# The last products of the feed-forward groups read 128 rows instead of 64, in an mLSTM and channel-mix kernel

## The chip, the core and the metric

The kernel runs on one core of a Trainium2 chip. The core has a matrix engine (TensorE, in the profile PE, with its weight loads as PEld), a vector engine (VectorE, DVE), a scalar engine (ScalarE, ACT), a general engine (GpSimd, POOL), and SyncE (SP), which here only issues DMA transfers. Each engine takes its instructions in the order of the program and waits on semaphores for the others. On-chip data lies in 128 partitions; TensorE multiplies a stationary operand, loaded first, by a moving one, sums over the partitions (the rows of the product), and writes to banks of PSUM. The metric is the device time of one execution in microseconds (us), and less is better.

## What is computed

The first half is a gated linear recurrence with a matrix state for each of 4 x 8 batches and heads, 768 steps, 40 channels a head. The second half is a feed-forward part over the 320 channels of all heads, with a shift by one token:

```python
C = f_stab[:, :, None, None] * C + i_stab[:, :, None, None] * np.einsum('bhd,bhe->bhde', vt, kt)
n = f_stab[:, :, None] * n + i_stab[:, :, None] * kt
h_tilde = np.einsum('bhde,bhe->bhd', C, qt)
denom = np.maximum(np.abs(np.einsum('bhd,bhd->bh', n, qt)[:, :, None]), 1.0)
y[:, :, t] = o * h_tilde / denom
...
xk = mu_k * x + (1.0 - mu_k) * x_prev
xr = mu_r * x + (1.0 - mu_r) * x_prev
k = np.maximum(xk @ w_k, 0.0)
v = k * k @ w_v
r = 1.0 / (1.0 + np.exp(-(xr @ w_r)))
return (r * v).astype(np.float32)
```

Here x is y with the heads side by side, 320 channels wide; w_k is 320 x 1024, w_v 1024 x 320, w_r 320 x 320.

## The kernel before

**Tiling.** The recurrence is cut into chunks of 128 tokens. Two chunks of one batch make a unit of 256 tokens, the step of the feed-forward part; there are 12 units, three per batch. Within a chunk the scores of all heads are products of q and k (`scores`, line 242), weighed by exponentials (`weigh`, 249); `inter` (263) takes what the state brings in, `intra` (283) what the chunk itself gives, `carry` (364) makes the state of the next chunk. `total`, `norm`, `gate`, `outcome` and `twin` finish the chunk's x on VectorE and GpSimd, and `turn` (394) transposes it, so that channels lie on the partitions.

**Two parts of each operand.** TensorE multiplies in a rounded float32 format (float32r), so each operand of the feed-forward part is kept as a high part, rounded to that format, and a low part, the rest. A product is then the sum of three: high by high, low x by high weights, high x by low weights. 320 channels are two tiles of 128 and one of 64. The tile of 64 is stored twice (`twin` for x, the host's `twice` for the weights), and `mix_l` (line 443) makes its third tile in one instruction with `nsel`, a column of 0 for the first 64 partitions and -1 for the others: rows 0 to 63 of `xl[:, 2]` hold the high part of x, rows 64 to 127 the low part. One product of `xl[:, 2]` and `wh[:, 2]` over 128 rows thus holds two of the three terms. The third, high x by low weights, is a product over 64 rows.

`terms` (line 491) lists these products: three for each of the first two tiles, two for the third, eight in all. `ffn_k` (498) makes two such groups for a pair of feature tiles, 16 products of 128x128 by 128x256, into one PSUM bank; there are four pairs a unit. `ffn_r` (534) makes one group of eight, 128 tokens by 320 channels, and runs twice a unit. `ffn_v` (552) has 24 products for each half unit, all over 128 rows. The weights come in as float64 bits and are taken apart on the chip by `size`, `guard`, `bits`, `parts` and `parts_l` in the first third of the program.

**What sets the order.** The order is written out by hand: the calls from line 576 on, each engine taking its part in that order. Units 0 and 1 are interleaved with the preparation of the weights. The loop from line 1062 on handles, for u from 2 to 11, the feed-forward part of unit u, the attention of unit n = u + 1, and the loads and the first scores of unit m = u + 2. On TensorE one pass is: `inter(n, 0)`, `ffn_k(u, 0)`, `intra(n, 0)`, `carry(n, 0)`, `ffn_k(u, 1)`, `scores(n, 1, ...)` twice, `turn(n, 0)`, `ffn_k(u, 2)`, `inter(n, 1)`, `intra(n, 1)`, `carry(n, 1)`, `ffn_r(u, 0)`, `ffn_k(u, 3)`, `ffn_r(u, 1)`, `turn(n, 1)`, `ffn_v(u)` twice, `scores(m, 0, ...)` twice. The first chunk of a batch has no `inter`, the last no `carry`.

**The scores' operands.** From unit 2 on they too are float32r: `split_h` (line 184, ScalarE) and `split_l` (191) take k and q apart, and `restack` (201) puts the parts above each other in tiles `k3` and `q3` of 120 rows by 18 transfers on SyncE's queue, nine for k and nine for q. There is one `k3` and one `q3`, so the transfers for unit m wait until `scores(n, 1, ...)` have read those of unit n. On SyncE a pass is: the output of unit u - 1, the loads of the output gate, q and k of unit m (lines 172, 160, 145), the 18 transfers, and one load of `e` (216).

Of the kernel before, what the change touches and what calls it, by code (L numbers as in the profile page):

```python
# [16 lines left out]
DM, DFF = H * D, 1024  # L17
P = 128
L = 128                # chunk of the recurrence
CPB = S // L           # chunks of a sequence  # L20
U = 256                # tokens of a unit of the feed-forward part
CPU = U // L
UPB = S // U
NU = B * UPB
UF = 2                 # units whose scores come from float32 products
E1 = D + 1             # a head's values with the column of ones
NF = DFF // P
BH = B * H
NEG = -1e30
# a float64 of 2**-127 has these upper 32 bits; read as a float32, such words keep their order  # L30
SMALL = struct.unpack("<f", struct.pack("<I", (1023 - 127) << 20))[0]
# [3 lines left out]
def mlstm_cmix_kernel(ctx: ExitStack, tc, qf, kf, qT, kT, kn, va, og, gi, gf, wk, wr, wv, mu, cmask, out):  # L35
# [8 lines left out]

# [1 line left out]
    gf_sb = p2.tile([BH, S], F32, bufs=1, name="gf_sb")  # L46
# [12 lines left out]

# [1 line left out]
    # M_t, less the sum of f up to t, is what every weight of the chunk is measured  # L61
    # from; R is the running maximum where the chunk starts.
    nm_dram = [dp.tile([BH, L], F32, name=f"nm_{c}") for c in range(CPB)]
# [49 lines left out]
    def columns(c):  # L113
        """the same with the chunk's tokens on the partitions"""
        ar, dg = rows[c]["ar"], rows[c].get("d")
        pt = ps.tile([P, 512], F32, tag="T", bufs=1, name="pt_g")
        for i in range(3):
            T.transpose(pt[:, i * BH:(i + 1) * BH], ar[:, i, :], ident[:BH, :BH])
        if dg is not None:
            T.matmul(pt[:3 * D, 3 * BH:4 * BH], ones[:, :3 * D], dg, start=True, stop=True)  # L120
        A.activation(acol[:, c, :], pt[:, 0:BH], AF.Copy)
        if c == 0:
            # nothing flows in from before the sequence: only the keys' scales
            A.activation(gk[:, c, 1, :], pt[:, 2 * BH:3 * BH], AF.Exp)
        else:
            A.activation(gk[:, c].rearrange("p i x -> p (i x)"), pt[:, BH:3 * BH], AF.Exp)
        if dg is not None:
            A.activation(dec[:, c, :], pt[:3 * D, 3 * BH:4 * BH], AF.Exp)

# [1 line left out]
    units = [{} for _ in range(NU)]  # L131

    def load_s(u, eng):
        if u >= NU:
            return
        t = units[u]
        if u < UF:
            # the first units' scores come from float32 products: nothing to wait for
            t["k3"] = p2.tile([D, H, U], F32, tag="k3", name="k0_sb", bufs=1)
            t["q3"] = p2.tile([D, H, U], F32, tag="q3", name="q0_sb", bufs=1)  # L140
            eng.dma_start(t["k3"], kf[u])
            eng.dma_start(t["q3"], qf[u])
        else:
            t["k"] = p2.tile([3 * D, 3, U], F32, name="k_sb", bufs=1)
            eng.dma_start(t["k"], kT[u])
# [16 lines left out]
    def load_o(u, eng):  # L162
        """the tile of the results of unit u - 2 and of unit u's output gate"""
        if u < 2:
            sg = p2.tile([P, 2 * CPU, DM], F32, name="sg")
            og_sb = units[u]["o"] = sg[:, :CPU, :]
            eng.dma_start(og_sb, og[u])
            return
        units[u - 2]["sg"] = p2.tile([P, 2 * CPU, DM], F32, name="sg")
        if u < NU:  # L170
            units[u]["o"] = units[u - 2]["sg"][:, CPU:, :]
            eng.dma_start(units[u]["o"], og[u])
# [3 lines left out]

    # float32r parts of q and k, stacked so that one product over 120 rows
    # holds kh*qh + kl*qh + kh*ql of a head
    def split_h(u, nm):
# [23 lines left out]

# [1 line left out]
    state = {}  # L205
# [20 lines left out]
    def exps(u, c, h0, h1):  # L226
        """exp(a_s - M_t) for s <= t, with s on the partitions"""
        if u >= NU:
            return
        t, b, cc, _, _ = where(u, c)  # L230
        e = t["e", c]
        for h in range(h0, h1):
            A.activation(e[:, h, :], e[:, h, :], AF.Exp, bias=acol[:, cc, b * H + h:b * H + h + 1])  # L233
# [17 lines left out]
    def inter(u, c):  # L251
        """from the earlier chunks"""
        if u >= NU:
            return
        t, _, cc, cs, _ = where(u, c)
        if cc == 0:
            return
        Cst = state["C"].rearrange("p h x -> p (h x)")
        pX = t["X", c] = ps.tile([P, 512], F32, tag="A", name="pX")
        for g in range(3):  # L260
            w = 3 if g < 2 else 2
            at = slice(g * 3 * E1, (g * 3 + w) * E1)
            T.matmul(pX[:, at], t["q"][:w * D, g, cs], Cst[:w * D, at], start=True, stop=True)  # L263
# [11 lines left out]
    def intra(u, c, h0=0, h1=H):  # L275
        """from this chunk"""
        if u >= NU:
# [19 lines left out]
    def norm(u, c, step):  # L297
        """1 / max(|n.q|, 1)"""
        if u >= NU:
# [33 lines left out]

    # the state of the next chunk
    def carry_in(u, c, eng):
# [51 lines left out]
    def turn(u, c):  # L387
        """to channels on the partitions; the last 64 channels twice"""
        if u >= NU:
            return  # L390
        t = units[u]
        pT = t["T", c] = ps.tile([P, 512], F32, tag="T", bufs=1, name="pT")
        for i in range(3):
            T.transpose(pT[:, i * P:(i + 1) * P], t["x", c][:, i * P:(i + 1) * P], ident)  # L394
# [13 lines left out]

# [1 line left out]
    def change(u, c, eng):  # L410
# [25 lines left out]
    def mix_l(u, nm, eng):  # L436
# [4 lines left out]
        xl = t["xl" + nm] = p2.tile([P, 3, U], F32R, tag="xl" + nm, name="xl" + nm, bufs=1)  # L441
        # rows 0..63: the high part, rows 64..127: the low part
        V.scalar_tensor_tensor(xl[:, 2, :], xh[:, 2, :].bitcast(F32), nsel, xm[:, 2, :], op0=ALU.mult, op1=ALU.add)  # L443
# [8 lines left out]
    def load_w(nm, i, slot, eng):  # L452
        """a piece of float64 weights: their bits, as pairs of words"""
        cut = slice(i * P, (i + 1) * P)
        wh, wl, src = (a[:, :, cut] if nm == "wk" else a[:, i:i + 1, :] for a in W[nm])
        # other spaces than "st" are those that the first unit has no use for yet
        st = p2.tile([*src.shape, 2], I32, tag=slot, name="wst", bufs=2 if slot == "st" else 1)
# [8 lines left out]
    def guard(nm, i, eng):  # L466
        """what is below float32's smallest normal number comes out as zero"""
        wf = pieces[nm, i]["wf"]
        eng.tensor_scalar(wf, wf, SMALL, None, op0=ALU.max)

    def bits(nm, i, step):
        """float32 of a float64: sign and top bit of the exponent stay; 7 bits of it and 23 of the fraction follow"""
        p = pieces[nm, i]
# [8 lines left out]
    def parts(nm, i):  # L482
        """the float32r parts"""
        p = pieces[nm, i]
# [6 lines left out]
    def terms(xh, xl, wh, wl):  # L491
        r = []
        for ct in range(2):
            r += [(xh, wh, ct, P), (xl, wh, ct, P), (xh, wl, ct, P)]
        r += [(xl, wh, 2, P), (xh, wl, 2, 64)]
        return r

    def ffn_k(u, pr):
# [3 lines left out]
        for i in range(2):  # L502
            f = 2 * pr + i
            for n, (xx, ww, ct, rows) in enumerate(tl):
                T.matmul(pk[:, i * U:(i + 1) * U], ww[:rows, ct, f * P:(f + 1) * P], xx[:rows, ct, :],  # L505
                         start=n == 0, stop=n == len(tl) - 1)

    def relu(u, pr):
        t = units[u]
        # the first unit's wait for wv while the second's pass  # L510
        r = t["r", pr] = p2.tile([P, 2, U], F32, tag="r0" if u == 0 else "rl", name="rl", bufs=2 if u else 4)
# [22 lines left out]
    def ffn_r(u, i):  # L534
        t = units[u]
        pr = t["pr", i] = bank(i, "pr")
        tl = terms(t["xhr"], t["xlr"], *W["wr"][:2])
        for m, (xx, ww, ct, rows) in enumerate(tl):
            T.matmul(pr[:, :DM], xx[:rows, ct, i * P:(i + 1) * P], ww[:rows, ct, :],  # L539
                     start=m == 0, stop=m == len(tl) - 1)  # L540
# [5 lines left out]
    def sigmoid(u):  # L546
        """of unit u's r and of unit u + 2's output gate"""
        sg = units[u]["sg"]
# [20 lines left out]

# [1 line left out]
    every = ExitStack()  # L571
    every.enter_context(tc.manual_schedule(engines=None))

    # the first unit's attention, while the weights come in; then its feed-forward part
    # @first
    gate_b(0)
# [483 lines left out]
    scores(3, 0, 0, "S")  # L1060
    # @last
    for u in range(2, NU):
        n, m = u + 1, u + 2
        # @body
        mix(u, "r")
# [94 lines left out]
        exps(m, 0, 6, 8)  # L1160
        # @tail
    result(NU - 1, 1)
# [68 lines left out]
```

## Time and profile before

| what | us |
|---|---|
| median of three runs | 424.5 |
| lowest and highest run | 422.74, 427.61 |
| span of the profiled execution | 427.9 |
| TensorE busy | 397.2 (93%) |
| VectorE busy | 302.4 (71%) |
| ScalarE busy | 235.3 (55%) |
| GpSimd busy | 183.0 (43%) |

Of the profiled execution only the span is given, from the first instruction to the last; it is 3.4 us above the median of the runs. In the rows of the profile, L505 is a line of the kernel and `out<-in` names the tiles; `64*128 64x256` is a stationary operand of 64 rows by 128 columns and a moving one of 64 rows by 256. The timeline gives the start and the duration in us, the engine (PE is TensorE's product, SPq and ACTq are transfers issued by SyncE and ScalarE), the line and the operation; `x16` merges 16 that follow each other; the bracket at the end is the time that the engine was idle before, and who ended it. A product's end is modelled, and consecutive products overlap in the array, so the distance of two starts tells what one costs, not its duration. In the row of the granted clock each digit is a fortieth of the span, 10.7 us, in tenths of full speed.

### The profile page before, as it was taken

The page shows a single profiled execution, that of the slowest core. Times are in us where ns is not written, and L with a number is a line of the kernel's source. Part 1 is how long each engine was busy: PE and PEld are TensorE (multiplying, and loading weights), DVE is VectorE, ACT ScalarE, POOL GpSimd, SP SyncE. Part 2 cuts the span into 40 slices and gives each one's busy share as a digit, 9 for nine tenths or more (in the row PEclk, how much of TensorE's full clock was granted, in tenths as well). Part 3 has the DMA queues.
Part 4 walks back from the last instruction along what each step waited for, and adds up shares of the span by engine and source line. Part 5 has one row for each costly group of instructions (what it writes and reads, how often), then busy time and mean ns, then how long its engine had stood idle before and what let it go on. Part 6 is the DMA issues. An engine that isn't in the chain of part 4 may idle for free.

```text
span 427.9 us, 7136 instructions
## 1 busy us (share of the span) xinstructions
PE 397.2 (93%) x2482; PEld 356.1 (83%) x2482; DVE 302.4 (71%) x589; ACT 235.3 (55%) x472; POOL 183.0 (43%) x204
## 2 busy tenths in 40 slices
PE   1874899878998999999999999999999999999996
PEld 0864788767888989989889889898899898998976
DVE  4366896699868677687677777876776778765611
ACT  3641553257636647638567566485476574763440
POOL 2355773676745361352452532613614426133040
PEclk9999999996589999999999999999999999999999
DMA  6867643547242464733835647448357465400000
GB/s 170 272 181 233 209 130 101 165 153 227 70 139 93 140 206 161 221 131 129 249 128 188 215 128 216 167 142 241 125 170 225 135 197 178 159 33 0 33 1 32
DMA packets 40022, 65.18 MB, mean 152 GB/s; under 512 B 3913, under 2 KB 26497, under 8 KB 39825
## 3 DMA queue, kind: packets, MB, share of 16 engines
q1 hardware_dynamic: 31836, 45.99, 34.5%
q10 hardware_dynamic: 8149, 18.72, 13.4%
q8 instruction: 20, 0.33, 0.3%
q14 instruction: 17, 0.14, 0.1%
HBM read 41.01 MB, written 4.03 MB: 105 GB/s over the span
## 4 chain that ended last, share of the span: by engine, by line
PE 67%; DVE 0%; issue 0%
PE pk L505 24%; PE pv L561 18%; PE pI L283 8%; PE pr L539 7%; PE pS L242 4%; PE pX L263 3%; PE pC L364 2%; PE pT L394 2%; DVE sg L566 0%
## 5 line engine op out<-in xcount | busy, mean ns | idle before, releaser
L505 PE MATMUL pk<-xhk,wkl 128*128 128x256 f32 (+1 forms) x288 | 96.4, 335 | 0.0
L505 PE MATMUL pk<-xlk,wkh 128*128 128x256 f32 x288 | 82.0, 297 | 0.7 <-DVE xlk L443 0.7
L512 ACT ACTIVATE rl<-pk 128x512 f32<-128x512 f32 x48 | 28.6, 597 | 92.3 <-PE pk L505 86.2
L505 PEld LDWEIGHTS pk<-xhk,wkl 128*128 128x128 f32 (+1 forms) x288 | 58.4, 203 | 14.0 <-issue 2.7
L505 PE MATMUL pk<-xhk,wkh 128*128 128x256 f32 x192 | 66.8, 348 | 0.0
L233 ACT ACTIVATE e<-e,acol 128x128 f32<-128x128 f32 x192 | 59.0, 389 | 5.7 <-POOL e L223 5.5
L561 PE MATMUL pv<-wvh,kh 128*128 128x320 f32 x192 | 60.5, 315 | 1.4 <-DVE sg L566 1.4
L223 POOL TENSOR_SCALAR_AFFINE_SELECT e<-e 128x1024 f32<-128x1024 f32 x24 | 27.0, 1128 | 77.9 <-DMA e<-nm 54.1
L505 PEld LDWEIGHTS pk<-xlk,wkh 128*128 128x128 f32 x288 | 59.4, 206 | 0.9 <-DVE xlk L443 0.9
L561 PE MATMUL pv<-wvl,kh 128*128 128x320 f32 x192 | 59.3, 309 | 0.0
L561 PE MATMUL pv<-wvh,kl 128*128 128x320 f32 x192 | 59.3, 309 | 0.0
L283 PE MATMUL pI<-va_sb,e 128*128 128x41 f32 x384 | 55.1, 309 | 1.8 <-DVE e L249 1.1
L283 PEld LDWEIGHTS pI<-va_sb,e 128*128 128x128 f32 x384 | 52.8, 219 | 4.2 <-DVE e L249 1.4
L522 POOL TENSOR_TENSOR kk<-rl 128x512 f32<-128x512 f32 x25 | 27.0, 1082 | 53.9 <-ACT rl L512 45.8
L505 PEld LDWEIGHTS pk<-xhk,wkh 128*128 128x128 f32 x192 | 39.2, 204 | 9.0 <-issue 3.0
L527 POOL TENSOR_TENSOR kl<-kk,kh 128x512 fp32r<-128x512 f32 x22 | 31.4, 1426 | 31.1 <-DVE kk L522 21.1
L561 PEld LDWEIGHTS pv<-wvh,kh 128*128 128x128 f32 x192 | 36.1, 188 | 1.9 <-DVE sg L566 1.6
L249 DVE TENSOR_TENSOR e<-pS,e 128x512 f32<-128x512 f32 x48 | 31.9, 679 | 7.9 <-PE pS L242 6.9
L561 PEld LDWEIGHTS pv<-wvl,kh 128*128 128x128 f32 x192 | 36.1, 188 | 0.0
L561 PEld LDWEIGHTS pv<-wvh,kl 128*128 128x128 f32 x192 | 36.0, 188 | 0.0
L426 DVE SCALAR_TENSOR_TENSOR xm<-xd,mu_sb,xT 128x256 f32<-128x256 f32 x72 | 35.5, 548 | 0.7
L522 DVE TENSOR_TENSOR kk<-rl 128x512 f32<-128x512 f32 x23 | 20.4, 886 | 17.4 <-ACT rl L512 17.4
(114 smaller groups left out, 786.4 us busy)
## 6 DMA issues: line engine op xcount, KB each, us to landing
e<-nm SPq DMA_DIRECT2D x13, 512.0 KB
e<-nm ACTq DMA_DIRECT2D x11, 512.0 KB
k<-sp_hk SPq DMA_DIRECT2D x40, 120.0 KB
q<-sp_hq SPq DMA_DIRECT2D x40, 120.0 KB
out<-sg SPq DMA_DIRECT2D x12, 320.0 KB
q_sb<-qT SPq DMA_DIRECT2D x10, 360.0 KB
va_sb<-va ACTq DMA_DIRECT2D x10, 328.0 KB
k_sb<-kT SPq DMA_DIRECT2D x9, 360.0 KB
```

The source lines that it names most:

```text
L223: G.affine_select(e, e, pattern=[[0, H], [1, L]], compare_op=ALU.is_ge, fill=NEG, base=0, channel_multiplier=-1)
L233: A.activation(e[:, h, :], e[:, h, :], AF.Exp, bias=acol[:, cc, b * H + h:b * H + h + 1])
L242: T.matmul(pS[:, hh * L:(hh + 1) * L], t["k3"][:, h, cs], t["q3"][:, h, cs], start=True, stop=True)
L249: V.tensor_tensor(ev, t["S", c, half], ev, op=ALU.mult)
L283: T.matmul(t["I", c][:, h * E1:(h + 1) * E1], t["e", c][:, h, :], t["va"][:, c, h * E1:(h + 1) * E1], start=True, stop=True)
L426: V.scalar_tensor_tensor(xm[:, ct, :], t["xd"][:, ct, :], mu_sb[:, i, ct:ct + 1], t["xT"][:, ct, :U], op0=ALU.mult, op1=ALU.add)
L505: T.matmul(pk[:, i * U:(i + 1) * U], ww[:rows, ct, f * P:(f + 1) * P], xx[:rows, ct, :], start=n == 0, stop=n == len(tl) - 1)
L512: A.activation(r.rearrange("p i t -> p (i t)"), t["pk", pr], AF.Relu)
L522: eng.tensor_tensor(kk, t["r", pr], t["r", pr], op=ALU.mult)
L527: eng.tensor_tensor(kl, t["kk", pr], t["kh", pr].bitcast(F32), op=ALU.subtract)
L539: T.matmul(pr[:, :DM], xx[:rows, ct, i * P:(i + 1) * P], ww[:rows, ct, :], start=m == 0, stop=m == len(tl) - 1)
L561: T.matmul(t["pv", i][:, :DM], xx[:, f % 2, ts], ww[:, f, :], start=f == 0 and n == 0, stop=f == NF - 1 and n == 2)
```

## The change

The last product of each group, until now `xh` by `wl` over rows 0 to 63 of the third tile, becomes `xl` by `wl` over all 128 rows. Rows 0 to 63 of `xl[:, 2]` are the high part of x, so this holds the same term; rows 64 to 127 add a further one, the low part of x by the low part of the weights. Those weight rows are there already, since the last 64 channels of the weights are stored twice and `parts_l` makes the low part of the whole tile. The number of rows goes out of the lists of `terms`, and the slices by it go out of the two loops. The other lines of the diff drop comments.

```diff
     def terms(xh, xl, wh, wl):
         r = []
         for ct in range(2):
-            r += [(xh, wh, ct, P), (xl, wh, ct, P), (xh, wl, ct, P)]
-        r += [(xl, wh, 2, P), (xh, wl, 2, 64)]
+            r += [(xh, wh, ct), (xl, wh, ct), (xh, wl, ct)]
...
+        r += [(xl, wh, 2), (xl, wl, 2)]
         return r
...
-            for n, (xx, ww, ct, rows) in enumerate(tl):
-                T.matmul(pk[:, i * U:(i + 1) * U], ww[:rows, ct, f * P:(f + 1) * P], xx[:rows, ct, :],
+            for n, (xx, ww, ct) in enumerate(tl):
+                T.matmul(pk[:, i * U:(i + 1) * U], ww[:, ct, f * P:(f + 1) * P], xx[:, ct, :],
                          start=n == 0, stop=n == len(tl) - 1)
...
-        for m, (xx, ww, ct, rows) in enumerate(tl):
-            T.matmul(pr[:, :DM], xx[:rows, ct, i * P:(i + 1) * P], ww[:rows, ct, :],
+        for m, (xx, ww, ct) in enumerate(tl):
+            T.matmul(pr[:, :DM], xx[:, ct, i * P:(i + 1) * P], ww[:, ct, :],
                      start=m == 0, stop=m == len(tl) - 1)
```

96 products of `ffn_k` and 24 of `ffn_r` are of that kind, 120 of TensorE's 2482. Each engine has as many instructions as before, in the same order. On TensorE, at the end of the first group of `ffn_k(0, 0)`, there stood (xhk and xlk are the high and low parts of x for the keys, wkh and wkl those of w_k):

```order
28 L505 MATMUL pk<-xlk,wkh 128x256
29 L505 MATMUL pk<-xhk,wkl 128x256
30 L505 MATMUL pk<-xlk,wkh 128x256
31 L505 MATMUL pk<-xhk,wkl 128x256
32 L505 MATMUL pk<-xhk,wkh 128x256
```

and now, two lines further down in the file:

```order
28 L507 MATMUL pk<-xlk,wkh 128x256
29 L507 MATMUL pk<-xhk,wkl 128x256
30 L507 MATMUL pk<-xlk,wkh 128x256
31 L507 MATMUL pk<-xlk,wkl 128x256
32 L507 MATMUL pk<-xhk,wkh 128x256
```

Row 31, the last of the group, reads xlk in place of xhk; nothing else moved.

## The prediction

> **What bounds the kernel now.** I read the page first, then the waits of TensorE, the chain of waits, busy time by stretch, the groups by form, and last the timelines of TensorE, SyncE and ScalarE in single units. The page, cut to three lines:
>
> ```profile
> span 427.9 us, 7136 instructions
> ...
> PEclk9999999996589999999999999999999999999999
> ...
> PE 67%; DVE 0%; issue 0%
> ```
>
> The waits of TensorE from 100 us to the end are one row (who waited for whom, us in total, times, longest). Two rows of busy time by stretch follow it: length, then busy us and instructions of PE, PEld, DVE, ACT, POOL, then the granted clock, the DMA share and GB/s.
>
> ```profile
> PE pv L561 <- DVE sg L566: 1.4, 1, 1.4
> ```
>
> ```profile
> 251.20:280.60 29.40, 29.40 (x208) 26.61 (x207) 22.73 (x45) 18.38 (x36) 11.56 (x13) 1.00 0.55 176
> 90.00:120.00 30.00, 28.84 (x127) 24.87 (x126) 28.08 (x51) 18.84 (x44) 21.91 (x21) 0.67 0.49 152
> ```
>
> After 100 us TensorE waits once, for 1.4 us. In one unit of the loop (251.2 to 280.6) it is busy all 29.40 us at full clock, while VectorE, the next busiest, has 22.73. The chain that ended last runs on TensorE almost alone. So a microsecond taken from TensorE's stream is a microsecond of time, until something else is late. Before the loop it is different: from 90 to 120 VectorE is busy 28.08 of 30 us and TensorE's clock averages 0.67.
>
> **What a product over 64 rows costs.** Busy time hides it, since a waiting array counts as busy. It shows in the starts. Timeline of TensorE in a unit (start, duration, then the operation):
>
> ```profile
> 260.31 0.28 PE L505 MATMUL pk<-xhk,wkl 128*128 128x256 f32 x1
> 260.43 0.28 PE L505 MATMUL pk<-xlk,wkh 128*128 128x256 f32 x1
> 260.64 0.38 PE L505 MATMUL pk<-xhk,wkl 64*128 64x256 f32 x1
> 260.95 0.39 PE L505 MATMUL pk<-xhk,wkh 128*128 128x256 f32 x1
> 261.17 0.28 PE L505 MATMUL pk<-xlk,wkh 128*128 128x256 f32 x1
> 261.29 0.29 PE L505 MATMUL pk<-xhk,wkl 128*128 128x256 f32 x1
> ...
> 261.98 0.38 PE L505 MATMUL pk<-xhk,wkl 64*128 64x256 f32 x1
> 262.29 1.98 PE L283 MATMUL pI<-va_sb,e 128*128 128x41 f32 x16
> ```
>
> Products over 128 rows start 0.12 us apart (260.31 to 260.43, 261.17 to 261.29). Around the 64-row product the three steps are 0.21, 0.31 and 0.22: 0.74 where 0.36 would do, so 0.38 us lost. Where a float32 product follows (262.29) I count only the two steps 0.21 and 0.31 against 0.24: 0.28. The receptance products, 320 wide, show the same:
>
> ```profile
> 275.16 0.31 PE L539 MATMUL pr<-wrl,xhr 128*128 128x320 f32 x1
> 275.31 0.30 PE L539 MATMUL pr<-wrh,xlr 128*128 128x320 f32 x1
> ...
> 276.11 0.28 PE L505 MATMUL pk<-xlk,wkh 128*128 128x256 f32 x1
> ```
>
> The three steps from 275.31 to 276.11 take 0.80 where 0.15 + 0.15 + 0.12 = 0.42 would do: 0.38 again. Is it the row count, or the place at the end of an accumulation group? The value products have group ends too, between 254.48 and 254.63:
>
> ```profile
> 254.34 0.31 PE L561 MATMUL pv<-wvl,kh 128*128 128x320 f32 x1
> 254.48 0.31 PE L561 MATMUL pv<-wvh,kl 128*128 128x320 f32 x1
> 254.63 0.31 PE L561 MATMUL pv<-wvh,kh 128*128 128x320 f32 x1
> 254.78 0.31 PE L561 MATMUL pv<-wvl,kh 128*128 128x320 f32 x1
> ```
>
> There the step is 0.15 as everywhere in that stage, so a group's end costs nothing and the row count is what is left.
>
> [...]
>
> **The change, part by part.** It adds and removes no instruction, and no engine's order changes. The last product of each group reads all 128 rows, and takes x from the tile that the product before it reads, so it waits for nothing new. Its own price: no row has this operand pair; the nearest is any 128-row product of the same width, 0.12 or 0.15 us, and a 64-row price of nothing extra is excluded by the rows above. I take 0.12 and 0.15. That the high part of x is released one product earlier (0.12 us) is worth nothing while ScalarE waits for VectorE there.
>
> A unit has eight 64-row products in its key part and two in its receptance part. Five key products are followed by products of the same kind (0.38 each) and three not (0.28): 2.74 us. The receptance pair adds 0.38 + 0.28. Together 3.4 us per unit, of about 29.
>
> What is late next: the scores of the unit after next. SyncE rebuilds k3 and q3 with 18 transfers per unit, and the loop closes on itself (scores, products, split on ScalarE, transfers, scores). Rows of three units, SyncE, TensorE and ScalarE apart:
>
> ```profile
> 269.51 4.88 SPq L201 DMA_DIRECT2D k<-sp_hk  x6
> 281.93 2.39 SPq L201 DMA_DIRECT2D q<-sp_lq  x3
> 311.67 2.39 SPq L201 DMA_DIRECT2D q<-sp_lq  x3
> 339.38 2.39 SPq L201 DMA_DIRECT2D q<-sp_lq  x3
> ```
>
> ```profile
> 287.53 0.34 PE L242 MATMUL pS<-q,k 120*128 120x128 f32 x2
> 316.28 0.34 PE L242 MATMUL pS<-q,k 120*128 120x128 f32 x2
> 344.97 0.45 PE L242 MATMUL pS<-q,k 120*128 120x128 f32 x3
> ```
>
> ```profile
> 268.65 0.83 ACT L184 ACTIVATE sp_hk<-k_sb 120x768 fp32r<-120x768 f32 x1
> 298.38 0.85 ACT L184 ACTIVATE sp_hk<-k_sb 120x768 fp32r<-120x768 f32 x1 [0.25 <-DMA k_sb<-kT]
> ```
>
> ```profile
> SPq L1225 <- DMA out<-sg: 1.8, 1, 1.8
> ```
>
> The last issue ends at 284.32, 314.06 and 341.77 (start plus 2.39), and the scores start at 287.53, 316.28 and 344.97: 3.21, 2.22 and 3.20 later. Part of that is the landing: above 0, at most 2.22 (the second unit did not wait); the nearest row is the wait for the last output to land, 1.8, which I take. Slack is then 1.41, 0.42 and 1.40 us, less than the 3.4 by which TensorE comes earlier. But the rebuilding starts earlier too: it follows the split (268.65 + 0.83, then 269.51), which follows the second pair of key products, and two pairs come before it in a unit: 2 x (0.38 + 0.28) = 1.3 us. Only if TensorE set the split: in the second unit it waited for the load of k (0.25), and then nothing is gained. So the units save 2.7, 0.4 to 1.7, and 2.7 us: 1.9 to 2.4 on average, of which I take 2.2. The rest, 1.2 us, becomes a wait of TensorE at the scores. Eight units have such a successor: 8 x 2.2 = 17.6. The last two have none: 2 x 3.4 = 6.8.
>
> Before the loop, 12 of the 96 key products run at the low clock:
>
> ```profile
> L505 PE MATMUL pk<-xhk,wkl 64*128 64x256 f32 x96 | 38.9, 405 | 0.0
> ```
>
> ```profile
> 112.68 0.41 PE L505 MATMUL pk<-xlk,wkh 128*128 128x256 f32 x1
> 113.02 0.58 PE L505 MATMUL pk<-xhk,wkl 64*128 64x256 f32 x1
> ...
> 113.91 0.41 PE L505 MATMUL pk<-xlk,wkh 128*128 128x256 f32 x1
> 114.12 0.41 PE L505 MATMUL pk<-xhk,wkl 128*128 128x256 f32 x1
> ```
>
> (12 because the mean 405 ns lies an eighth of the way from 380 to 580.) There the three steps from 112.68 take 1.23 against 3 x 0.21: 0.60 lost, 1.04 in a pair, 6.2 in six pairs; two further pairs and four receptance groups at 0.66 and 0.33 add 2.6. How much of these 8.8 us counts depends on VectorE, which waits for TensorE at two late places:
>
> ```profile
> 83.56 0.50 DVE L374 TENSOR_TENSOR Cn<-pC,cm_sb 120x328 f32<-120x328 f32 x1 [2.38 <-PE pC L364]
> 122.46 0.50 DVE L293 TENSOR_TENSOR t<-pI,t 128x328 f32<-128x328 f32 x1 [2.31 <-PE pI L283]
> ```
>
> Bounds 0 and 8.8; between these waits VectorE is nearly full (28.08 of 30), so I take the two waits: 4.7.
>
> Sum: 17.6 + 6.8 + 4.7 = 29.1 us. The span of the profiled execution, 427.9, becomes 398.8; the runs' median is 424.5, so 395.4, say 395.
>
> **The rivals.**
> - All of it comes through: the landing takes less than 1.8 us and the split always follows TensorE. 8 x 3.4 + 6.8 + 4.7 = 38.7, so 386. Against it: slack of 2.22 us at most in the second unit is below 3.4.
> - The load of k sets every split, as at 298.38; then only the slack is saved, (1.41 + 0.42 + 1.40)/3 = 1.1 per unit: 8.6 + 6.8 + 4.7 = 20.1, so 404. Against it: one row in three shows that wait.
> - The change does nothing: 64 rows cost what 128 cost, and the loss belongs to something else in those places that stays, the group's end for one. Then the sum is 0 and the time 424.5. The rows at 254.48 speak against it.
> - Slower: the new waits at the scores lower TensorE's clock. The rows ahead of the slow stretch:
>
> ```profile
> 97.11 0.38 PE L505 MATMUL pk<-xlk,wkh 128*128 128x256 f32 x1 [0.66 <-DVE xlk L443]
> 99.64 0.28 PE L283 MATMUL pI<-va_sb,e 128*128 128x41 f32 x1 [0.50 <-DVE e L249]
> ```
>
> Two short waits, then 0.67 of the clock over 30 us: some 20 us at half. Steps are 0.21 there against 0.12, so such a stretch costs 20 x (1 - 0.12/0.21) = 8.6 us. One gives 404, and from four on (34.4 against 29.1) the kernel is slower: 430 and more. Against it: the 1.4 us wait after 100 us was followed by full clock. [...]
>
> **How the numbers follow.** The forecast 0.55, all through 0.12, load of k 0.18, no effect 0.05, clock 0.10 (one or two stretches 0.06, three 0.01, four or more 0.03). From 385 to 406 lie the forecast, the second rival, half of the first and one stretch of low clock: about 0.82. About 1% is what a measurement of this kernel can tell from no change. Faster by more: 0.55 + 0.12 + 0.18 + 0.06 = 0.91; within 1%: 0.06; slower: 0.03.
>
> **What would show it.** After: steps of 0.12 and 0.15 us through every key and receptance group; a pair of key products in about 1.9 us; a unit of about 26.7 us; TensorE waiting about 1 us per unit for the rebuilt k or q at its scores, and no longer 29.40 of 29.40 busy. Steps still above 0.2 around the last product would refute the first step; no wait at the scores would give the first rival; a clock below 1 after 135 us the last.

## The result and the profile after

| | median, us | lowest and highest, us |
|---|---|---|
| kernel before, same chip | 426.01 | 422.74, 427.61 |
| changed kernel | 400.97 | 398.64, 403.43 |

The ratio is 0.950, with a 95% interval of 0.938 to 0.962: faster by 25 us, inside the range of the prediction, 6 us above its number. The profiled execution took 403.43 us. Four lines of its page follow: span, busy time, granted clock, and the chain that ended last by engine.

```profile
span 401.6 us, 7136 instructions
...
PE 347.7 (87%) x2482; PEld 336.8 (84%) x2482; DVE 317.4 (79%) x589; ACT 234.4 (58%) x472; POOL 190.2 (47%) x204
...
PEclk9999999958779999999999999999989999999999
...
PE 39%; DMA 8%; DVE 6%; ACT 5%; SPq 4%; issue 3%; POOL 2%; ACTq 0%; POOLq 0%
```

TensorE holds 39% of the chain, where it held 67%. In the row of the clock the low slices before the loop remain, and one 8 stands in the loop, at 291 to 301 us. Busy time by stretch for eight units of the loop, in the kernel before and then in the changed one; the stretch begins with the fifth of a chunk's eight score products and ends with the first of such a chunk, at the same two places of both programs (length, then busy us and instructions of PE, PEld, DVE, ACT and POOL, then the granted clock):

```profile
143.05:374.35 231.30, 231.30 (x1617) 209.02 (x1616) 174.42 (x338) 145.58 (x276) 88.51 (x98) 1.00 0.56 178
```

```profile
135.02:355.08 220.06, 206.96 (x1616) 202.19 (x1615) 186.93 (x338) 144.91 (x276) 92.17 (x98) 0.99 0.57 185
```

TensorE's stream got 231.30 - 206.96 = 24.3 us shorter, and 220.06 - 206.96 = 13.1 us of it came back as waits: 11.2 us are left. The 26.3 us of span (427.9 - 401.6) divide so, by these starts:

| part | predicted, us | measured, us |
|---|---|---|
| up to the scores at 143.05, now 135.02 | 4.7 | 8.0 |
| eight units | 17.6 | 11.2 |
| the rest, from 374.35, now 355.08 | 6.8 | 7.0 |

Timeline of TensorE in a unit of the changed kernel:

```profile
261.15 0.28 PE L507 MATMUL pk<-xlk,wkh 128*128 128x256 f32 x1
261.27 0.28 PE L507 MATMUL pk<-xlk,wkl 128*128 128x256 f32 x1
261.39 0.31 PE L541 MATMUL pr<-wrh,xhr 128*128 128x320 f32 x1
261.53 0.30 PE L541 MATMUL pr<-wrh,xlr 128*128 128x320 f32 x1
...
262.26 0.31 PE L541 MATMUL pr<-wrh,xlr 128*128 128x320 f32 x1
262.40 0.30 PE L541 MATMUL pr<-wrl,xlr 128*128 128x320 f32 x1
263.80 0.44 PE L394 MATMUL pT<-ident,x 128*128 128x128 f32 x2 [1.09 <-POOL x L326]
264.91 0.33 PE L394 MATMUL pT<-ident,x 128*128 128x128 f32 x1 [0.68 <-DVE x L332]
```

The step around the last key product (`xlk,wkl`) is 0.12 us and around the last receptance product 0.15, as the prediction took them. What is new stands in the brackets: the transposes of the unit's second chunk wait 1.09 + 0.68 us. The waits of TensorE from 130 us on (who waited for whom: us in total, times, longest):

```profile
PE pT L394 <- POOL x L326: 6.0, 5, 1.9
PE pT L394 <- DVE x L332: 5.4, 8, 0.7
PE pS L242 <- DMA q<-sp_lq: 0.8, 3, 0.3
PE pC L364 <- ACT xT L406: 0.7, 1, 0.7
```

The scores, where the prediction had put the new wait, wait 0.8 us in all. The transposes, which did not wait in the loop before, wait 11.4. Why they do is in the chain of waits, here from one unit into the next (start, duration, what; "issue" is time for which no releaser shows):

```profile
273.83 0.49 DVE sg L568
...
274.37 0.37 SPq L570
...
275.78 7.60 DMA k_sb<-kT
...
283.49 0.86 ACT sp_hk L184
...
284.36 0.51 DVE sp_lk L191
...
285.73 1.10 DVE kk L524
...
288.54 1.84 POOL sp_lq L191
...
291.25 0.82 POOL x L326
...
292.09 1.09 DVE x L332
...
293.23 0.33 PE pT L394
```

SyncE's queue issues the output of the unit before (L570) only when VectorE has made it (`sg`), and the loads of the next unit stand behind it. The load of k lands 7.6 us later, and ScalarE splits k then. VectorE takes the low part (`sp_lk`, from 284.36 us), and the work of the second chunk, which stands behind it in VectorE's order, starts at 285.24. GpSimd's product `x` follows, behind its split of q (`sp_lq`, 1.84 us), then VectorE's copy (`twin`), then the transpose. ScalarE's wait for this load is one row of its waits in the changed kernel, after 130 us (in the kernel before it was 0.2 us, once):

```profile
ACT sp_hk L184 <- DMA k_sb<-kT: 6.3, 5, 2.4
```

The copy is a second lengthening. The groups by form, of the kernel before and then of the changed one (count, busy us, mean ns):

```profile
L332 DVE COPY x<-x 128x64 f32<-128x64 f32 x11 | 2.1, 194 | 5.9 <-POOL x L326 5.9
```

```profile
L332 DVE COPY x<-x 128x64 f32<-128x64 f32 x11 | 10.8, 979 | 5.9 <-POOL x L326 5.8
```

The same copy went from 0.19 to 0.98 us in the mean, and the transpose behind it waits for it in eight passes, up to 0.7 us each: the 5.4 us above. Timeline of GpSimd and VectorE in the unit shown above:

```profile
263.70 1.04 POOL L524 TENSOR_TENSOR kk<-rl 128x512 f32<-128x512 f32 x1
263.77 1.08 DVE L332 COPY x<-x 128x64 f32<-128x64 f32 x1 [0.51 <-POOL x L326]
```

It starts behind GpSimd's square (`kk`) and ends 0.1 us after it. In the kernel before the square came behind the copy (308.15 and 307.89 us in such a unit), when its input `rl` was ready later. There the copy took 0.20 us; beside the square it takes 1.08. What makes it longer isn't shown by these rows.

### The profile page after: what moved, and what is told of

Read it like the earlier page. It is cut to its first block, busy times and chain, and to the rows that moved or that the text cites. A ratio compares the mean times of both kernels' runs of the same rounds, so it can differ in the third digit from the quotient of the medians.

```text
span 401.6 us, 7136 instructions
## 1 busy us (share of the span) xinstructions
PE 347.7 (87%) x2482; PEld 336.8 (84%) x2482; DVE 317.4 (79%) x589; ACT 234.4 (58%) x472; POOL 190.2 (47%) x204
## 4 chain that ended last, share of the span: by engine, by line
PE 39%; DMA 8%; DVE 6%; ACT 5%; SPq 4%; issue 3%; POOL 2%; ACTq 0%; POOLq 0%
PE pk L507 13%; PE pv L563 13%; DMA k_sb<-kT 5%; PE pI L283 5%; SPq L201 3%; PE pr L541 3%; PE pS L242 3%; PE pC L364 2%; PE pX L263 1%; ACT e L233 1%; DMA q<-sp_lq 1%; POOL x L326 1%; DVE x L332 1%; ACT rl L514 1%; DMA e<-nm 1%
## 5 line engine op out<-in xcount | busy, mean ns | idle before, releaser
L507 PE MATMUL pk<-xlk,wkh 128*128 128x256 f32 x288 | 79.7, 290 | 0.5 <-DVE xlk L443 0.5
L223 POOL TENSOR_SCALAR_AFFINE_SELECT e<-e 128x1024 f32<-128x1024 f32 x24 | 30.5, 1272 | 97.2 <-DMA e<-nm 91.9
L507 PE MATMUL pk<-xhk,wkh 128*128 128x256 f32 x192 | 59.0, 307 | 0.0
L507 PEld LDWEIGHTS pk<-xlk,wkh 128*128 128x128 f32 x288 | 57.2, 199 | 0.7 <-DVE xlk L443 0.7
L507 PE MATMUL pk<-xhk,wkl 128*128 128x256 f32 x192 | 55.9, 291 | 0.0
L283 PE MATMUL pI<-va_sb,e 128*128 128x41 f32 x384 | 52.7, 301 | 3.6 <-DVE e L249 2.3
L283 PEld LDWEIGHTS pI<-va_sb,e 128*128 128x128 f32 x384 | 51.6, 215 | 4.6 <-DVE e L249 1.7
L524 POOL TENSOR_TENSOR kk<-rl 128x512 f32<-128x512 f32 x25 | 27.8, 1113 | 31.2 <-ACT rl L514 24.3
L529 POOL TENSOR_TENSOR kl<-kk,kh 128x512 fp32r<-128x512 f32 x22 | 33.5, 1523 | 14.8 <-DVE kk L524 8.4
L507 PEld LDWEIGHTS pk<-xhk,wkl 128*128 128x128 f32 x192 | 38.1, 199 | 0.0
L394 PE MATMUL pT<-ident,x 128*128 128x128 f32 x72 | 15.8, 307 | 25.8 <-DVE x L326 7.8
```

The lines of the kernel that those rows point to most:

```text
L223: G.affine_select(e, e, pattern=[[0, H], [1, L]], compare_op=ALU.is_ge, fill=NEG, base=0, channel_multiplier=-1)
L283: T.matmul(t["I", c][:, h * E1:(h + 1) * E1], t["e", c][:, h, :], t["va"][:, c, h * E1:(h + 1) * E1], start=True, stop=True)
L507: T.matmul(pk[:, i * U:(i + 1) * U], ww[:, ct, f * P:(f + 1) * P], xx[:, ct, :], start=n == 0, stop=n == len(tl) - 1)
L524: eng.tensor_tensor(kk, t["r", pr], t["r", pr], op=ALU.mult)
L529: eng.tensor_tensor(kl, t["kk", pr], t["kh", pr].bitcast(F32), op=ALU.subtract)
```

## The experiments

**Is it the row count? 96 rows.** The last product reads 96 rows instead of 128. It leaves out low x by low weights for 32 of the last 64 channels.

```diff
-        r += [(xl, wh, 2), (xl, wl, 2)]
+        r += [(xl, wh, 2, P), (xl, wl, 2, 96)]
```

> The changed kernel, but the last product of each group reads 96 rows (of the third tile rows 0 to 95), not 128. Theory 1, the loss belongs to the form of 64 rows: steps around the last product stay 0.12 and 0.15 us, the time is that of the changed kernel, about 401 us (ratio 0.95). Theory 2, any product over fewer rows than the one before it costs the restart: steps of 0.21, 0.31 and 0.22 us come back, the time is that of the kernel before, about 425 us.

Measured: 401.15 us, ratio 0.950 (0.941 to 0.960), the changed kernel's own. Its timeline of TensorE:

```profile
250.51 0.28 PE L507 MATMUL pk<-xlk,wkh 128*128 128x256 f32 x1
250.62 0.28 PE L507 MATMUL pk<-xlk,wkl 96*128 96x256 f32 x1
250.74 0.28 PE L507 MATMUL pk<-xhk,wkh 128*128 128x256 f32 x1
```

Steps of 0.11 and 0.12: reading fewer rows than the neighbours cost nothing by itself here. The first theory holds, and the extra time belongs to the form with 64.

**Two 64-row products side by side.** In the kernel before, the second group of each key pair begins with its 64-row product, so that the two of a pair are neighbours. The result stays the same sum.

```diff
-            for j, (...) in enumerate(tl):
+            for j, (...) in enumerate(tl[-1:] + tl[:-1] if i else tl):
```

> The kernel before, with its 64-row products, but in the second group of each pair of key groups the 64-row product comes first instead of last, so that two of them stand side by side. Theory 1, the cost is in going from 128 rows to 64 and back: a pair has two such passages instead of four, saves about 0.28 us, 4 x 0.28 = 1.1 us a unit, and the time falls by some 8 to 12 us, to about 415. Theory 2, every 64-row product has its own price: nothing falls, 426 us, and the second of two neighbours starts 0.3 us after the first.

Measured: 409.54 us, ratio 0.969 (0.961 to 0.977). Its timeline of TensorE:

```profile
250.53 0.28 PE L505 MATMUL pk<-xlk,wkh 128*128 128x256 f32 x1
250.74 0.50 PE L505 MATMUL pk<-xhk,wkl 64*128 64x256 f32 x2
251.16 0.39 PE L505 MATMUL pk<-xhk,wkh 128*128 128x256 f32 x1
251.39 0.28 PE L505 MATMUL pk<-xlk,wkh 128*128 128x256 f32 x1
```

Four steps take 0.86 us where 4 x 0.12 = 0.48 would do: 0.38 is lost, once for two products. So the price is paid in passing from the form with 128 rows to that with 64 and back, not for each product. Not one 64-row product less runs here, and two thirds of the change's gain are there: 16.6 us against 426.15, the median of the kernel before that was measured with it. That is more than the first theory expected, since the stage before the loop gains in full (the scores that started at 143.05 us start at 134.29).

**One product less.** The changed kernel without the last product of each group. It leaves out high x by low weights for the last 64 channels.

```diff
-        r += [(xl, wh, 2), (xl, wl, 2)]
+        r += [(xl, wh, 2)]
```

> The changed kernel without the last product of each group; left out is the high part of x by the low weights of the last 64 channels. That takes 8 x 0.12 + 2 x 0.15 = 1.3 us of TensorE's work from each of 12 units. Theory 1, in the loop TensorE now waits for the x of the second chunk at the transposes (turn): there nearly nothing is gained, only the stage before the loop and the last unit give 2 to 4 us, about 398 us, and the waits at the transposes grow by about 1 us a unit. Theory 2, TensorE's own work still sets the time: 12 x 1.3 = 15 us less, about 386 us.

Measured: 399.39 us, ratio 0.945 (0.936 to 0.954): 96 products of 0.12 us and 24 of 0.15, 15 us in all, are gone, and the time is within 2 us of the changed kernel's. Its longest row of TensorE's waits from 130 us on:

```profile
PE pT L394 <- POOL x L326: 12.4, 8, 2.2
```

The transposes wait for GpSimd's `x` twice as long (12.4 against 6.0), and the eight units take 351.60 - 132.45 = 219.2 us against 220.1. The loop is no longer set by TensorE; the chain ahead of the transpose sets it, as the first theory had it. A part of the missing gain is the clock's: this profile has three stretches of 3.4 us at half clock in the loop where the changed kernel's has one (mean granted clock 0.951 against 0.966), some 3 us more (3.4 x (1 - 0.15/0.26) = 1.4 us each).

**The copy on GpSimd.** In the changed kernel the second chunk's copy is made by GpSimd, behind the product that it reads.

```diff
-        twin(n, 1, V)
+        twin(n, 1, G)
```

> The changed kernel, but in the loop the copy of the second chunk's last 64 channels (twin) is GpSimd's, right behind the product that makes them, instead of VectorE's. In the changed kernel VectorE's copy takes 1.08 us beside GpSimd's square, and the third transpose waits 0.68 us in each pass. Theory 1, these transposes set the loop: that wait goes, 0.5 to 0.7 us a pass, and the time falls by 3 to 6 us to 395 to 398 us. Theory 2, the rebuilding of k and q for the scores sets it (the forecast's): the wait moves to the scores, which then wait about 0.7 us a pass, and the time stays at 401 us.

Measured: 400.69 us, ratio 0.948 (0.938 to 0.958): no gain where the first theory expected one. The wait for the copy is gone, but the one for `x` stays, and the scores wait 2.1:

```profile
PE pT L394 <- POOL x L326: 7.8, 6, 2.7
```

The copy alone isn't the cause. This profile too has three stretches of 3.4 us at half clock in the loop (mean granted clock 0.947), so a gain of some 3 us may be hidden behind them.

**The load of k early.** In the changed kernel SyncE issues the load of k at the head of the pass, ahead of the output that waits for VectorE.

```diff
         n, m = u + 1, u + 2
 
+        load_s(m, SY)
         mix(u, "r")
...
         gate(n, 0, V)
-        load_s(m, SY)
```

> The changed kernel, but in the loop SyncE issues the load of k for unit m at the head of the pass, ahead of the output of unit u - 1 and the loads of the output gate and q, where it waits for nothing of this pass. In the changed kernel ScalarE waits 6.3 us in all, in 5 passes, for that load before it splits k, and the chain of the longest pass goes through it. Theory 1, the load of k sets the loop: that wait goes to 0, and the time falls by 4 to 8 us to 393 to 397 us. Theory 2, it is only one of several things that are late together: the wait goes, the waits at the transposes stay within 3 us of the 13.7 us of the changed kernel, the time stays at 399 to 402 us.

Measured: 393.51 us, ratio 0.933 (0.930 to 0.937), the time that the first theory gave. ScalarE's row for `k_sb` is gone from its waits after 130 us. Waits of TensorE there:

```profile
PE pT L394 <- DVE x L332: 5.4, 8, 0.7
PE pT L394 <- POOL x L326: 3.1, 5, 1.2
PE pS L242 <- DMA q<-sp_lq: 0.5, 2, 0.4
```

But 8.5 us of waits are left at the transposes, of 11.4; that they would fall by less than 3 us is what the second theory had. The load is one of several links. The eight units take 345.52 - 131.69 = 213.8 us by the starts of the scores, against 220.1 in the changed kernel and 216.6 and 219.0 in two further executions (the repeat below and the one with 96 rows).

**The rebuilding late.** The changed kernel with the copy on GpSimd and, so that GpSimd's `x` comes sooner, the low part of q, all nine transfers of q and the load of `e` behind them moved behind `square(u, 3, G)`.

```diff
-        split_l(m, "q", G)
-        restack(m, "q", SY)
-        fetch_m(m, 1, SY)
...
-        twin(n, 1, V)
+        twin(n, 1, G)
...
         square(u, 3, G)
+        split_l(m, "q", G)
+        restack(m, "q", SY)
+        fetch_m(m, 1, SY)
```

> The changed kernel with the copy twin on GpSimd as in the run before, and in the loop GpSimd's split of q (1.84 us, beside which VectorE's 8-element maximum takes 1.77 us) moved behind the second chunk's x and the last square. Theory 1, the chain from the second chunk's sums through VectorE and GpSimd to the transposes sets the loop: it gets shorter by 1.5 to 2 us a pass, the waits at the transposes nearly vanish, the time falls to 390 to 394 us. Theory 2, the rebuilding of k and q sets it: the transposes stop waiting, but the scores wait 1 us or more a pass, and the time stays above 397 us.

Measured: 411.47 us (403.84 to 414.76), without a ratio, since the runs lie too far apart. The theory that it would gain fell: the lowest run, too, is above the changed kernel's 400.97. The profile is of the highest run, 414.76. Waits of TensorE from 130 us on, and its stretch to 412:

```profile
PE pS L242 <- DMA q<-sp_lq: 7.3, 16, 1.1
PE pC L364 <- ACT xT L406: 3.1, 2, 2.8
PE pT L394 <- POOL x L326: 1.2, 2, 0.6
```

```profile
130.00:412.00 282.00, 265.56 (x1974) 260.26 (x1972) 207.26 (x380) 167.59 (x324) 113.45 (x123) 0.95 0.47 150
```

The wait that the prediction had put at the scores appears here, because the rebuilding was made late; and the clock averages 0.95 over 282 us, some 27 us of them at half (four stretches in the timeline, of 3.4, 6.8, 13.7 and 3.4 us). With steps of 0.21 us for 0.12 there, the clock costs 27 x (1 - 0.12/0.21) = 12 us, about what parts this run from the lowest. That the transposes wait 1.2 us for `x`, against 7.8 with the copy moved alone, speaks for GpSimd's split of q as a further link of their chain; it isn't shown, since TensorE now also comes to them later, by its waits at the scores.

**Load, copy and rebuilding together**, and the same three moves on the kernel before. The edits are those of the last two experiments, the early load and the late rebuilding.

> The changed kernel with all three moves: load of k at the head of the pass, twin on GpSimd, split of q behind the last square. Theory 1, both chains that end at TensorE get shorter, so TensorE sets the loop again: waits after 130 us under 5 us in all, units of about 25.6 us, 382 to 388 us. Theory 2, the rebuilding of k and q (18 issues, 14.8 us) is a floor of its own: the scores wait about 1 us a pass, 392 us or more.

> The kernel before, with its 64-row products, and the same three moves. Theory 1, in the kernel before TensorE hides both chains: the moves gain nothing beyond 1%, 422 to 428 us. Theory 2, the moves are worth something by themselves: as much as between the changed kernel and its version with the three moves.

Measured: 393.89 us on the changed kernel, ratio 0.931 (0.923 to 0.938), no better than the early load alone: the transposes no longer wait, the scores do (6.2 us, 16 times), as the second theory had it. On the kernel before 427.04, ratio 1.014 (1.009 to 1.018): slightly slower. While TensorE's own stream is longer than these chains, moving them gains nothing; what they are worth now was opened by the change.

**The changed kernel again, the load with the copy, and a version to keep.** The last one also splits the high part of k ahead of `relu(u, 1)` on ScalarE, now that the load lands early.

```diff
+        split_h(m, "k")
         relu(u, 1)
...
         inter(n, 1)
-        split_h(m, "k")
```

> The changed kernel once more, as the measure for the two runs beside it: 399 to 403 us by both theories. If short stretches at half clock come with long waits of TensorE, its profile shows them only right behind passes in which the transposes waited 2 us or more.

> The changed kernel with the load of k at the head of the pass and the copy twin on GpSimd, the split of q left in its place. Theory 1, the transposes alone still set the loop: 388 to 391 us, since the 5.4 us that they wait for VectorE's copy in the run with the early load go. Theory 2, the rebuilding of k and q for the scores is as late as they are (its last transfer lands within 0.4 us of the scores in that run): the time stays at 392 to 395 us and the scores wait about 0.5 us a pass.

> The same with one more move: ScalarE splits k ahead of the relu of the second pair of key products, not behind its square, so that the 18 transfers start as soon as the scores have read the old tiles, about 1.2 us earlier. Theory 2, the rebuilding sets the loop: its last transfer lands 1 us earlier, the scores stop waiting, and the time falls to 383 to 388 us. Theory 1, the transposes set it: no more than 2 us against the run beside it.

Measured together: the changed kernel 400.17 us, ratio 0.941 (0.929 to 0.954); load and copy 392.19, ratio 0.926 (0.915 to 0.936); with the split 389.19 (386.62 to 393.0), ratio 0.917 (0.906 to 0.928). The repeat had one short stretch of half clock, behind waits of 1.07 + 0.68 us, less than the 2 us that were expected ahead of one. In the load with the copy the eight units take 342.91 - 132.11 = 210.8 us; the wait for the copy is gone, the transposes still wait 3.4 us for `x`, and the scores now wait 1.4 us (6 times). The last version starts the rebuilding sooner by the early split. Its waits of TensorE after 130 us:

```profile
PE pT L394 <- POOL x L326: 4.4, 4, 1.5
```

It lies just above what the second theory gave it, 3.0 us below load and copy. Its scores never wait, and the eight units take 340.44 - 131.54 = 208.9 us; 8 x 3.4 less than before would be 231.3 - 27.2 = 204.1. This version beats both kernels: 37 us below the kernel before that was measured with it (426.48).

## Why the prediction was right in sign and too large by four microseconds

**The price of a 64-row product** (0.38 us, or 0.28 ahead of a float32 product) was right. The steps became 0.12 and 0.15; 96 rows cost as little as 128; and two 64-row products side by side share one price. In the best version, whose loop has no stretch of low clock, TensorE is busy 203.6 of the 208.9 us of eight units, 27.7 less than 231.3, where 8 x 3.4 = 27.2 was taken. The rival that the change does nothing is refuted. What costs is the change between the two forms (0.38 us, once for a single product and once for two side by side), not the number of rows.

**8 x 2.2 = 17.6 for the loop** measured 11.2, and this is the step that failed, in its last sentence: "The rest, 1.2 us, becomes a wait of TensorE at the scores." I followed one chain, the rebuilding of k and q, took its slack as what limits the gain, and left the others unpriced. The one that was late first ends at the second chunk's transpose: load of k, split on ScalarE, low part on VectorE with the chunk's normalization queued behind it, the product `x` on GpSimd, copy, transpose. The waits there came to 11.4 us over the loop, and 0.8 at the scores. Taking away the load's part gave 7 us by medians (393.51 against 400.97 and 400.17), which were measured beside different medians of the kernel before; by the ratios, 0.933 against 0.950 and 0.941, it is 3 to 7 us. By the traces it is 2.8 to 6.3 us of the eight units, and 219.0 - 213.8 = 5.2 against the run with 96 rows, where neither has a stretch of low clock. The copy on top gave 213.8 - 210.8 = 3.0 there, and nothing that could be seen by itself, with the load still late and more low clock. What makes the transposes wait for `x` with the load early (3.1 us, and 3.4 with the copy moved too) wasn't separated; GpSimd's split of q is the next suspect.

My chain was not wrong, only second: with the transposes' chain shortened the scores wait (1.4 us, and 6.2 with the rebuilding moved back, which makes it later by itself), and with the split early no wait is left at the scores.

**Rivals.** "The load of k sets every split" had the right mechanism and the wrong reach: it gave 404 by way of the rebuilding, in every unit, while the load delayed ScalarE in 5 passes and, in the unit whose chain is shown, did its harm by VectorE's queue. That all comes through is refuted for the change alone; the best version comes within 4.8 us of it in the eight units. The clock did fall behind new waits, in stretches of 3.4 to 13.7 us and not of 20: one of 3.4 in the profiled execution, at about 1.4 us, and 27 us in the kernel with the late rebuilding. In its profile the change alone lost little by it.

**Before the loop** 4.7 was taken and 8.0 measured, inside its bounds of 0 and 8.8. The two pairs of key products between 67 and 82 us went in steps of 0.21 us before, the step at half clock (0.21 at 113.91); now they run between 66 and 73 us in steps of 0.12. The row of the clock doesn't show this (1.00 from 66 to 82 us in the kernel before), and up to 93 us it can't be relied on: in the kernel before the receptance products go in steps of 0.27 up to 93.05 us and of 0.15 from 93.28 on, both under a 9. VectorE, which I had counted as the cover, is busy 39.8 of the 40 us from 60 to 100 us, where it was 33.2. That it got its inputs earlier is what I take from it; no run shows it alone. Every kernel without the lone 64-row key products has the scores that started at 143.05 us at 131.5 to 135.0, and the other one with them at 139.37. What brings the short steps sooner there wasn't tried by itself.

**The last units**, 6.8, measured 7.0, with the end of the program. That the sum, 29.1, came within 3 us of the 26.3 of span is in part luck: 6.4 us too much in the loop stand against 3.3 too little before it.

## What to carry to other kernels

Where a stream of 128-row products is broken by single ones of 64 rows, read the steps between their starts: the loss doesn't show in busy time (29.40 us of 29.40 with it), and filling the rows with data that is there removed it here, and putting two such products side by side left one price for the two. When the bounding engine gets faster, list every chain that ends in it and their slacks, with what is queued in order behind each instruction that waits; the gain ends at the shortest of them, and the next one is close behind. A move that gains nothing before a change can be worth several microseconds after it, so try the moves again.

## What the runs showed of the hardware that I had not expected

Half clock of TensorE followed short waits. Timeline of TensorE in the changed kernel, and the busy time of the stretch behind it:

```profile
292.11 0.44 PE L394 MATMUL pT<-ident,x 128*128 128x128 f32 x2 [1.88 <-POOL x L326]
293.23 0.33 PE L394 MATMUL pT<-ident,x 128*128 128x128 f32 x1 [0.68 <-DVE x L332]
...
294.30 0.47 PE L563 MATMUL pv<-wvh,kl 128*128 128x320 f32 x1
294.56 0.47 PE L563 MATMUL pv<-wvh,kh 128*128 128x320 f32 x1
...
297.42 0.31 PE L563 MATMUL pv<-wvh,kl 128*128 128x320 f32 x1
297.57 0.30 PE L563 MATMUL pv<-wvh,kh 128*128 128x320 f32 x1
```

```profile
293.90:297.30 3.40, 3.40 (x15) 3.40 (x14) 2.42 (x6) 3.37 (x4) 0.00 (x0) 0.50 0.43 141
```

The steps go from 0.26 back to 0.15 after 3.4 us. Two waits of 2.56 us in all stood ahead of it here, 1.75 us in the repeat, while 1.09 + 0.68 = 1.77 us at 263.80 were followed by full clock (1.00 from 265 to 290 us). So the sum of the waits doesn't decide alone, and no run here shows what else does.

Two small operations of VectorE took about as long as GpSimd's beside them. The copy has been shown (1.08 us beside 1.04); a maximum over 8 elements took 1.77 us, ending with GpSimd's split of q, where the same one takes 0.17 in a unit's first chunk (at 250.50 us). It did so in the kernel before as well (1.75 us at 275.07), so the change didn't bring it. GpSimd's and VectorE's timelines of the changed kernel:

```profile
260.23 1.84 POOL L191 TENSOR_TENSOR sp_lq<-q_sb,sp_hq 120x768 fp32r<-120x768 f32 x1
260.33 1.77 DVE L309 TENSOR_TENSOR den<-t,den 128x8 f32<-128x8 f32 x1
```
